# Thresholded attention followed by a leaky-ReLU feed-forward layer: plain DMAs moved from SyncE's queue to GpSimd's, and PV five steps behind the scores in place of four

## The chip, the cores and the metric

The kernel runs on one core of a Trainium2 chip. The metric is the device time of one execution in microseconds (us); the median of several runs is compared. Beside the runs there is one profiled execution, from which every duration of a single instruction comes. The engines are TensorE (PE in the profile; PEld are its weight loads), VectorE (DVE), ScalarE (ACT), GpSimd (POOL) and SyncE (SP), which only issues DMAs here.

## What is computed

The reference, cut to what matters (batch 8, heads 8, sequence 576, head dimension 64, d_model 512, d_ff 2048, tau 0.02):

```python
scores = scale * np.matmul(q, k.transpose(0, 1, 3, 2))
thresh = np.max(scores, axis=-1, keepdims=True) - tau
scores = np.where(scores >= thresh, scores, -1000000000.0)
attn = np.exp(scores - np.max(scores, axis=-1, keepdims=True))
attn = attn / (np.sum(attn, axis=-1, keepdims=True) + 1e-09)
o = np.matmul(attn, v)                 # 8, 8, 576, 64
x = o.transpose(0, 2, 1, 3).reshape(8 * 576, 512)
h = x @ w_in
out = np.maximum(0.01 * h, h) @ w_out  # 4608, 512 in float32
```

## The kernel before

**Steps.** The attention is cut into 144 steps, 18 for each batch. A step is one batch b, one column group c and one pair p. The query rows are split over five column groups: c = 0 to 3 have four steps each, and c = 4 has two. In the last batch the order of the groups is 0, 1, 4, 2, 3. The order of all instructions is written out by hand: the loop at L435 runs over steps s, and each engine executes its own instructions in the order in which the loop emits them. Semaphores are placed where one engine needs another's data or a buffer that is still in use.

**What one step does.** TensorE computes the scores of step s in PSUM (L300, 36 matmuls with q as the weights). VectorE copies them out with their maxima (`smax`, L354, twice), computes the thresholded P for one head (L474) while ScalarE does the other (L476). In the next step VectorE clamps P (L461), ScalarE takes the exponentials into a tile w (L465, four buffers, NW), VectorE writes the reciprocal sums beside them (L480, L481), and `turn_w` (L368) has SyncE issue a DMA that transposes w into wt. LAG steps after the scores, TensorE multiplies wt by v (`pv`, L319). After the last pair of a column group VectorE scales the result out of PSUM (L331, or L336 for c = 4), which makes one group's x ready.

wt is a tile of four slots, one for each pair of a column group, with two buffers (NWT). Its slot 0 is written first; the buffer is free when PV and the evacuation of the column group two before are done.

**The feed-forward layer.** Each group of 128 tokens gives four units of h (16 matmuls, L201, then a ReLU on ScalarE, L214) and four units of o (4 or 5 matmuls). Units wait in two queues, hq and oq, and the loop takes about one of each in a step. At the end of a group, ScalarE copies the output to osb (L243, three buffers), and the store (L244) is issued at the head of the next step. After the loop, a tail works off the units that are left, and VectorE copies their outputs (L241).

**Preparing q and k.** For high precision, q and k are split into a high and a low 16-bit part. `load_half` (L79) loads half of a batch's heads (576 KB) into km or qm. `hi` (L138, on ScalarE) makes the high part, `x64` (L144) and `lo` (L150) on GpSimd make the low part, and `turn` (L154) has SyncE issue a DMA transpose to kst or qst. This is done one batch ahead; the steps at which each part is emitted stand in L389 to L409. GpSimd's arithmetic and its loads of v and of the layer's weights are each made to wait for VectorE's instruction at L461 in the same step (`after_anchor`, L89). Batch 0 is prepared ahead of the loop, with the low part on VectorE.

**DMA queues.** All transposes, the loads of q and k and the stores are issued by SyncE; v, w_in and w_out are loaded by GpSimd. In each step the order on SyncE's queue is: a store, if there is one; turn_w of the step before; then what the table of steps holds (loads, turns). On GpSimd's queue it is what the table of steps holds, in the order in which the table was filled.

Of the kernel before, what the change touches and what calls it, by code (L numbers as in the profile page):

```python
# [16 lines left out]
def kernel(  # L17
# [20 lines left out]
    nc = tc.nc  # L38
# [3 lines left out]
    DM = moe_w_in.shape[0]  # L42
    DF = moe_w_in.shape[1]
    C = 1.0 / (64.0 * 64.0 * 8.0)
    LAG = 4
    L1_GROUPS = set(range(8, 36))
    WIO = 20
    NJ = DF // 128
# [30 lines left out]
    def load_half(src, store, nm, b, hb):  # L79


        m = store[b, hb] = sb.tile([128, 2, 576], FP32, tag=nm, bufs=2, name=nm)
        nc.sync.dma_start(
            out=m, in_=src[b, :, :, :].rearrange("(h f) (p t) d -> f p h (t d)", h=2, t=9)[
                ds(2 * hb, 2)].rearrange("f p h x -> (f p) h x"))

# [112 lines left out]
    tail = [False]  # L199
    def mm(out_, lhsT, rhs, start, stop):  # L200
        nc.tensor.matmul(out=out_, lhsT=lhsT, rhs=rhs, start=start, stop=stop, skip_group_check=True)  # L201
# [21 lines left out]
    def o_unit(G, c):  # L223
        if c == 0:
            n = len(late) % 3 if tail[0] else 2
            late.append(0)
            if n < 2:
                G.op = ps.tile([128, 4, 256], FP32, tag=f"sc{n}", bufs=1, name="op")[:, 0:2, :].rearrange("p a b -> p (a b)")
            else:
                G.op = ps.tile([128, 512], FP32, tag="o", bufs=1, name="op")  # L230
        if G.l1:
            mm(G.op, G.x[:, c, :], w_io16[:, c, :], c == 0, False)
        for j in range(4 * c, 4 * c + 4):
            mm(G.op, G.g[:, j, :], w_out16[:, j, :], j == 0 and not G.l1, j == NJ - 1)
        if c == 3:
            op = G.op

            def fin():
                osb = sb.tile([128, 512], FP32, tag="osb", bufs=3, name="osb")
                if tail[0]:  # L240
                    nc.vector.tensor_copy(out=osb, in_=op)  # L241
                else:
                    nc.scalar.activation(out=osb, in_=op, func=AF.Copy, bias=0.0, scale=1.0)  # L243
                return lambda: nc.sync.dma_start(out=G.rows, in_=osb)  # L244
            return fin
        return None

# [60 lines left out]
    def pv(s):  # L308
        b, c, p = steps[s]
        wt = st[s]["wt"]  # L310
        vt = vts[b]
        n = 128 if c < 4 else 64
        if p == 0:
            pvt[0] = ps.tile([128, NP, n], FP32, tag="pv", bufs=1, name="pv")
        pvp = pvt[0]
        for u in range(1 if c < 4 else 2):
            for j in range(5):
                for h in range(2):
                    nc.tensor.matmul(  # L319
                        out=pvp[ds(64 * h, 64), p + u, :], lhsT=vt[:, p + u, h, j, :],  # L320
                        rhs=wt[:, 4 * h + j, ds(64 * u, n)],
                        start=(j == 0), stop=(j == 4), skip_group_check=True, tile_position=(0, 64 * h))
        last = p == (NP - 1 if c < 4 else NP - 2)
        G, col, done = group_of(b, c)

        def evac():


            if c < 4:
                x_ = G.x.rearrange("f g (p i) -> f g i p", i=2)  # L330
                nc.vector.tensor_tensor(  # L331
                    out=x_, in0=pvp.rearrange("f g (i p) -> f g i p", i=2),
                    in1=wts[0][:, :, 9, :].rearrange("f g (i p) -> f g i p", i=2), op=AX.mult)
            else:
                x_ = G.x.rearrange("f g (p i) -> f g i p", i=2)[:, :, col // 64, :]
                nc.vector.tensor_tensor(  # L336
                    out=x_.rearrange("f (a u) p -> f a u p", u=2),
                    in0=pvp.rearrange("f (a u) p -> f a u p", u=2),
                    in1=wts[0][:, 0:2, 9, :].rearrange("f a (u p) -> f a u p", u=2), op=AX.mult)
            if done:  # L340
                for u in range(4):
                    hq.append((h_unit(G, u), u))

        wts = [st[s]["wt4"]]
        return evac if last else None
# [31 lines left out]
    for hb in range(2):  # L377
        load_half(k, kms, "km", 0, hb)
        load_half(q, qms, "qm", 0, hb)
# [9 lines left out]
    for b in range(1, B):  # L389
        s0 = 18 * (b - 1)  # L390
        for hb in range(2):
            t0 = s0 + PREP + 8 * hb
            at(t0 - 5, lambda b=b, hb=hb: load_half(k, kms, "km", b, hb))
            at(t0 - 3, lambda b=b, hb=hb: load_half(q, qms, "qm", b, hb))
            at(t0 - 1, lambda b=b, hb=hb: hi("k", b, hb))
            at(t0 + 2, lambda b=b, hb=hb: hi("q", b, hb))
            i = 0
            for nm in "kq":
                for h in range(2):
                    at(t0 + i, lambda nm=nm, h=h, b=b, hb=hb: after_anchor(x64(nm, b, hb, h)))  # L400

                    def f(nm=nm, h=h, b=b, hb=hb):
                        for part in PARTS[nm]:
                            after_anchor(lo(nm, b, hb, h, part))
                    at(t0 + i + 1, f)
                    i += 2
                at(t0 + i, lambda nm=nm, b=b, hb=hb: turn(nm, b, hb))
        for i in range(4):
            at(s0 + PREP + 6 + i, lambda b=b, i=i: load_v(b, i))  # L409
# [24 lines left out]
    stores = []  # L434
    for s in range(NS + LAG + 1):  # L435
        live = s < NS
# [21 lines left out]
        if 0 < s <= NS:  # L458
# [5 lines left out]
            for h in range(2):  # L464
                nc.scalar.activation(  # L465
                    out=e["W"][:, ds(576 * h, 576)], in_=e["P"][:, h, :], func=AF.Exp, bias=exp_bias, scale=1.0,
                    accum_out=sm[:, h : h + 1])
        if live:
# [6 lines left out]
                out=d["P"][:, 0, :], in0=sa, scalar1=ma, scalar2=tau_f, op0=AX.subtract, op1=AX.add)  # L475
            nc.scalar.activation(out=d["P"][:, 1, :], in_=sB, func=AF.Identity, bias=bb, scale=1.0)  # L476
        leak()
        if 0 < s <= NS:
# [3 lines left out]
                out=e["W"][:, 1152:1280].rearrange("p (h r) -> p h r", h=2),  # L482
                in0=rc.unsqueeze(2).to_broadcast([128, 2, 64]), scalar1=1.0, scalar2=None, op0=AX.mult)
            turn_w(s - 1)
        evac = None
        if 0 <= s - LAG < NS:
            evac = pv(s - LAG)
        for i, o in enumerate(ou):
# [65 lines left out]
```

## Time and profile before

| What | Value |
|---|---|
| median of 9 runs | 629.73 us (619.21 to 632.48) |
| profiled execution | 626.12 us, span from first to last instruction 624.3 us |
| mean granted TensorE clock in it | 0.969 |
| PE busy | 521.1 us, 83% |
| DVE busy | 445.4 us, 71% |
| ACT busy | 441.9 us, 71% |
| POOL busy | 146.1 us, 23% |
| DMA queue of SyncE (q1, hardware) | 96.50 MB, its packets 86.9% of 16 engines' span |
| DMA queue of GpSimd (q0, software) | 8.92 MB, 11.2% |

A line of a timeline gives the start in us, the length in us, engine, line of the kernel, operation, output<-input and the number of merged instructions; a bracket gives the engine's idle time before it and what ended that. A line of the waits gives who waited for whom, the total in us, how often, and the longest. SPq is SyncE's queue; the length of a DMA there is the time to issue it, not the time to land. The shares of the two DMA queues add up to more than their engines' time where packets of both are under way at once.

### The profile page before, as it was taken

The page shows a single profiled execution, that of the slowest core. Times are in us where ns is not written, and L with a number is a line of the kernel's source. Part 1 is how long each engine was busy: PE and PEld are TensorE (multiplying, and loading weights), DVE is VectorE, ACT ScalarE, POOL GpSimd, SP SyncE. Part 2 cuts the span into 40 slices and gives each one's busy share as a digit, 9 for nine tenths or more (in the row PEclk, how much of TensorE's full clock was granted, in tenths as well). Part 3 has the DMA queues.
Part 4 walks back from the last instruction along what each step waited for, and adds up shares of the span by engine and source line. Part 5 has one row for each costly group of instructions (what it writes and reads, how often), then busy time and mean ns, then how long its engine had stood idle before and what let it go on. Part 6 is the DMA issues. An engine that isn't in the chain of part 4 may idle for free.

```text
span 624.3 us, 23173 instructions
## 1 busy us (share of the span) xinstructions
PE 521.1 (83%) x9840; PEld 374.7 (60%) x9840; DVE 445.4 (71%) x1385; ACT 441.9 (71%) x950; POOL 146.1 (23%) x196
## 2 busy tenths in 40 slices
PE   0442569897897989989897989899998989999997
PEld 0332456664465757767575766676676767677764
DVE  4563459887478878878785878777886868888810
ACT  3352448776468769879786878878887878888831
POOL 0362412123121242124321232124212332000000
PEclk9999979899799889999998999999998989999999
DMA  8899999999969799999999899969998999897821
GB/s 228 186 132 211 205 148 160 209 182 192 189 102 215 128 210 175 219 166 200 197 180 188 152 194 190 219 123 225 189 196 153 208 188 151 154 112 128 128 63 51
DMA packets 299048, 106.90 MB, mean 171 GB/s; under 512 B 273856, under 2 KB 286144, under 8 KB 298944
## 3 DMA queue, kind: packets, MB, share of 16 engines
q1 hardware_dynamic: 285888, 96.50, 86.9%
q0 software_dynamic: 13056, 8.92, 11.2%
q8 instruction: 77, 1.26, 0.9%
q14 instruction: 27, 0.22, 0.1%
HBM read 36.70 MB, written 9.44 MB: 74 GB/s over the span
## 4 chain that ended last, share of the span: by engine, by line
PE 54%; DMA 28%; DVE 12%; ACT 2%; SPq 2%; issue 2%; ACTq 0%; DVEq 0%
DMA wt<-w 20%; PE op L201 19%; PE hp L201 14%; PE sc L300 13%; DMA qst<-qs 7%; PE pv L319 6%; DVE sf L354 6%; PE wiop L201 2%; SPq L156 2%; DVE gT L196 1%; DVE xT L331 1%; DVE P L461 1%; DVE P L474 1%; DMA qm<-in_q_dram 1%; DMA km<-in_k_dram 1%
## 5 line engine op out<-in xcount | busy, mean ns | idle before, releaser
L354 DVE TENSOR_SCALAR_CACHE_REDUCE sf<-sc 128x576 f32<-128x576 f32 x288 | 206.6, 755 | 114.9 <-PE sc L300 113.7
L465 ACT ACTIVATE w<-P 128x576 f16<-128x576 f16 x288 | 193.6, 675 | 26.5 <-DVE P L461 18.3
L300 PE MATMUL sc<-kst,qst 64*64 64x192 f16 x5184 | 147.6, 258 | 42.5 <-DMA kst<-ks 16.2
L201 PEld LDWEIGHTS <-win 128*128 128x128 f16 x2304 | 145.6, 100 | 35.0 <-issue 3.2
L476 ACT ACTIVATE P<-sf,bb 128x576 f16<-128x576 f32 x144 | 111.4, 773 | 70.4 <-DVE bb L472 65.1
L201 PE MATMUL hp<-xT,win 128*128 128x128 f16 x2304 | 157.5, 223 | 0.0
L201 PE MATMUL op<-wout,gT 128*128 128x512 f16 x576 | 152.8, 389 | 0.1
L300 PEld LDWEIGHTS <-qst 64*64 64x64 f16 x5184 | 114.0, 112 | 60.8 <-DMA qst<-qs 32.7
L214 ACT ACTIVATE gT<-hp 128x512 f16<-128x512 f32 x144 | 85.2, 592 | 53.3 <-PE hp L201 50.8
L319 PE MATMUL pv<-wt,v 128*64 128x128 f16 (+1 forms) x1600 | 71.6, 225 | 55.8 <-DMA wt<-w 49.0
L319 PEld LDWEIGHTS <-v 128*64 128x64 f16 x1600 | 51.5, 114 | 76.9 <-issue 54.8
L201 PEld LDWEIGHTS <-gT 128*128 128x128 f16 x576 | 54.8, 100 | 53.9 <-issue 5.5
L474 DVE TENSOR_SCALAR P<-sf,mx 128x576 f16<-128x576 f32 x144 | 73.8, 513 | 0.0
L461 DVE TENSOR_SCALAR P<-P 128x1152 int16<-128x1152 int16 x144 | 66.2, 460 | 9.1 <-ACT P L476 4.0
L150 POOL TENSOR_TENSOR ks<-km,ks 128x320 f16<-128x320 f32 (+1 forms) x56 | 40.1, 736 | 88.6 <-DVE P L461 75.5
L150 POOL TENSOR_TENSOR qs<-qm,qs 128x576 f16<-128x576 f32 x28 | 35.8, 1280 | 86.7 <-DVE P L461 68.5
L465 ACT ACTIVATION_READ_ACCUMULATOR w<-P 128x1 f32 x288 | 54.7, 190 | 0.0
L144 POOL TENSOR_SCALAR km<-km 128x576 f32<-128x576 f32 x28 | 18.8, 672 | 147.0 <-ACT ks L138 101.3
L201 PE MATMUL op<-wio,xT 128*128 128x512 f16 x112 | 44.5, 397 | 0.8 <-ACT osb L243 0.8
L481 DVE TENSOR_SCALAR w<-rc 128x128 f16<-128x128 f32 x144 | 32.9, 229 | 5.0
L144 POOL TENSOR_SCALAR qm<-qm 128x576 f32<-128x576 f32 x28 | 18.8, 672 | 57.1 <-DVE P L461 57.1
L331 DVE TENSOR_TENSOR xT<-pv,wt 128x512 f16<-128x512 f32 x32 | 23.4, 731 | 10.0 <-PE pv L319 10.0
(28 smaller groups left out, 232.7 us busy)
## 6 DMA issues: line engine op xcount, KB each, us to landing
km<-in_k_dram SPq DMA_DIRECT2D x16, 576.0 KB, 5.6
qm<-in_q_dram SPq DMA_DIRECT2D x16, 576.0 KB, 5.5
out_dram<-osb SPq DMA_DIRECT2D x36, 256.0 KB, 4.1
v<-in_v_dram POOLq DMA_DIRECT2D x16, 160.0 KB, 5.8
wt<-w SPq DMA_TRANSPOSE x144, 4.7
v<-in_v_dram POOLq DMA_DIRECT2D x16, 128.0 KB, 5.6
win<-in_moe_w_in_dram POOLq DMA_DIRECT2D x8, 256.0 KB, 13.8
wout<-in_moe_w_out_dram POOLq DMA_DIRECT2D x8, 256.0 KB, 10.4
```

What stands on the lines that cost most here:

```text
L144: return nc.gpsimd.tensor_scalar(out=m, in0=m, scalar1=64.0, scalar2=1.0, op0=AX.mult, op1=AX.mult)
L150: return nc.gpsimd.tensor_tensor(out=dst[:, h], in0=src[:, h], in1=h_[:, h], op=AX.subtract)
L201: nc.tensor.matmul(out=out_, lhsT=lhsT, rhs=rhs, start=start, stop=stop, skip_group_check=True)
L214: nc.scalar.activation(out=gv, in_=hp, func=AF.Relu, bias=0.0, scale=0.99)
L300: nc.tensor.matmul(out=sc[h][ds(64 * u, 64), part, 0:192], lhsT=qsts[b, hb][r, qi, 2 * c + u if c < 4 else 8, ds(64 * g, 64)], rhs=ksts[b, ...
L319: nc.tensor.matmul(out=pvp[ds(64 * h, 64), p + u, :], lhsT=vt[:, p + u, h, j, :], rhs=wt[:, 4 * h + j, ds(64 * u, n)], start=(j == 0), sto ...
L354: nc.vector.tensor_scalar(out=thirds(sf), in0=sc[:, 0:3, 0:192], scalar1=C, scalar2=None, op0=AX.mult, op1=AX.max, accum_out=mx)
L461: anchor[0] = nc.vector.tensor_scalar(out=pi, in0=pi, scalar1=NEG, scalar2=None, op0=AX.max)
L465: nc.scalar.activation(out=e["W"][:, ds(576 * h, 576)], in_=e["P"][:, h, :], func=AF.Exp, bias=exp_bias, scale=1.0, accum_out=sm[:, h : h ...
L474: nc.vector.tensor_scalar(out=d["P"][:, 0, :], in0=sa, scalar1=ma, scalar2=tau_f, op0=AX.subtract, op1=AX.add)
L476: nc.scalar.activation(out=d["P"][:, 1, :], in_=sB, func=AF.Identity, bias=bb, scale=1.0)
L481: nc.vector.tensor_scalar(out=e["W"][:, 1152:1280].rearrange("p (h r) -> p h r", h=2), in0=rc.unsqueeze(2).to_broadcast([128, 2, 64]), sca ...
```

## The change

The loads of q and k for batches 1 to 7 (28 DMAs) and all stores that are issued in the loop or right behind it (33 of 36) are issued by GpSimd's queue; the loads of batch 0, the last stores in the tail and all transposes stay on SyncE. They are not tied to L461. PV runs five steps behind the scores, so that the loop has one step more. Buffer counts and the steps at which loads are emitted stay as they are.

```diff
-    LAG = 4
+    LAG = 5
...
         m = store[b, hb] = sb.tile([128, 2, 576], FP32, tag=nm, bufs=2, name=nm)
-        nc.sync.dma_start(
+        (nc.sync if b == 0 else nc.gpsimd).dma_start(
             out=m, in_=src[b, :, :, :].rearrange("(h f) (p t) d -> f p h (t d)", h=2, t=9)[
                 ds(2 * hb, 2)].rearrange("f p h x -> (f p) h x"))
...
-                return lambda: nc.sync.dma_start(out=G.rows, in_=osb)
+                return lambda: (nc.sync if tail[0] else nc.gpsimd).dma_start(out=G.rows, in_=osb)
```

## The prediction

> **What bounds the kernel now.** I read the chain that ended last first, then the waits in total, then two batches side by side, then SyncE's queue at one stall. The chain, by engine and line:
>
> ```profile
> PE 54%; DMA 28%; DVE 12%; ACT 2%; SPq 2%; issue 2%; ACTq 0%; DVEq 0%
> DMA wt<-w 20%; PE op L201 19%; PE hp L201 14%; PE sc L300 13%; DMA qst<-qs 7%; PE pv L319 6%; DVE sf L354 6%; PE wiop L201 2%; SPq L156 2%; DVE gT L196 1%; DVE xT L331 1%; DVE P L461 1%; DVE P L474 1%; DMA qm<-in_q_dram 1%; DMA km<-in_k_dram 1%
> ```
>
> TensorE is the bound for over half the span, and two transposes by DMA interrupt it: wt (the softmax weights, for PV) and qst (the queries, for the scores). The waits (us in total, times, longest) size that:
>
> ```profile
> PE pv L319 <- DMA wt<-w: 49.0, 19, 7.1
> ...
> PE sc L300 <- DMA qst<-qs: 16.1, 6, 3.7
> ...
> ACT w L465 <- DMA wt<-w: 7.5, 2, 4.6
> ```
>
> Of the 49.0 us, six waits before 83 us make 29.5, two near 150 us make 4.7, and the others, 2.6 us at most, make 14.8. Each of the six for qst stands at the third step of a batch.
>
> Batches 6 and 7 as stretches (start and end, length, busy time of PE, PEld, DVE, ACT, POOL, then clock, DMA share, GB/s); during batch 7 nothing is loaded for a next one:
>
> ```profile
> 462.85:531.21 68.36, 63.78 (x1228) 45.48 (x1226) 52.74 (x168) 54.55 (x119) 18.91 (x24) 0.95 1.03 178
> 531.21:589.25 58.04, 57.09 (x1182) 41.41 (x1181) 49.35 (x159) 48.69 (x108) 0.00 (x0) 1.00 0.82 133
> ```
>
> Batch 7 makes 17 step intervals in 58.04 us with TensorE 98% busy; its undisturbed step is 3.35 us. Eighteen of these are 60.3 us, and batches 2 to 6 take 65.2 to 69.4. TensorE's work is the floor, and about 7 us a batch are stalls on it. SyncE's queue ahead of batch 6's stall, and TensorE at it:
>
> ```profile
> 462.49 0.57 SPq L83 DMA_DIRECT2D qm<-in_q_dram  x1
> 463.24 1.58 SPq L368 DMA_TRANSPOSE wt<-w  x1
> 464.91 4.84 SPq L156 DMA_TRANSPOSE qst<-qs  x1
> ...
> 471.81 0.94 PE L300 MATMUL sc<-kst,qst 64*64 64x192 f16 x36 [2.20 <-DMA qst<-qs]
> ...
> 473.49 1.91 PE L201 MATMUL op<-wout,gT 128*128 128x512 f16 x4
> 475.20 1.72 PE L201 MATMUL hp<-xT,win 128*128 128x128 f16 x16
> ...
> 478.38 1.03 PE L201 MATMUL op<-wout,gT 128*128 128x512 f16 x4
> ```
>
> A load of q goes into the queue 2.4 us ahead of the critical transpose, which then takes 6.85 us to land where an uncontended one (161.53 us) took 4.8. The bracket is TensorE's wait. A stall also costs afterwards: the same four matmuls take 1.91 us behind it and 1.03 a step later, 16 of hp 1.72 in place of 1.06, together 1.5 us more.
>
> **The change, part by part.** The sum is made against the profiled execution: 626.1 us, its span 624.3. The median shown is 629.7, so 3.6 us more.
>
> *PV a step later.* No instruction is added but one drain step. Each wt gets one step, 3.35 us, more until TensorE needs it. Not all of that counts: w has four buffers, so the exponentials of step s+4 (L465) need the transpose of step s landed too, and they start some 0.5 us before PV would now. I take 2.8 us. That covers each of the 14.8 us of small waits and most of the two near 150 us (0.7 and 4.0); with the slow matmuls after three of them, some 6 us, 25.5 us is the most. The startup waits (29.5 us) I leave out: the w buffers hold ScalarE to the same landings there, as its two waits show. The transfers remain and can be late again, so I take 21, bounds 10 and 25.5.
>
> *Loads through GpSimd's queue.* 28 loads of 576 KB leave SyncE. In the trace GpSimd ends the qs subtraction of that step at 458.60 us; its queue then holds the load, which so goes out 3.9 us before SyncE's 462.49. Such a load landed 5.5 us after issue at the median, so it is nearly out of qst's way. Without any load ahead, at the start of batch 7, qst still landed 0.95 us late; that stays. The six waits and the slow matmuls behind five of them (7.5 us by the lengthened next steps) are 23.6 us; less six times 0.95 it is 17.9 at most. At least nothing, if the transfers meet anyway. I take 11, nearer the upper row, because the issue moves by more than the stall.
>
> *SyncE's issue time.* 28 loads at 0.6 us and 33 stores at 0.58 leave a queue that issues for 50 to 58 us of each 65 to 69 us batch. That is some 36 us off SyncE, and shows through the transposes' landing alone, so it is in the two terms above.
>
> *The start.* Now SyncE issues batch 1's first km at 19.88 us, behind the four first turns, and ScalarE waits 4.07 us for it. GpSimd's queue is empty then: it can issue when km's first buffer is free, near 11.4. The first wt then goes some 2.5 us earlier, and the weight loads behind it. Against that, the two loads' 32 packets for each DMA engine (93 ns each in the packet records) are 3 us, and fall among the turns that start the scores. Gain 2.5, bounds -3 and +5.
>
> *GpSimd's work.* 61 DMAs at 0.66 us are 40 us; GpSimd goes from 146 to 186 us busy, hidden in an engine that idles 77% of the time. The meeting with VectorE is not hidden by itself. The nearest rows:
>
> ```profile
> L474 DVE TENSOR_SCALAR P<-sf,mx x144: 507/510/641, 19.4 to 591.8; 128x576 f16<-128x576 f32 x144
> ...
> L461 DVE TENSOR_SCALAR P<-P x144: 440/460/722, 20.4 to 593.2; 128x1152 int16<-128x1152 int16 x144
> ...
> L108 POOL DMA_DIRECT2D v<-in_v_dram x32: 617/658/843, 26.4 to 502.8; - x32
> ```
>
> (min/median/max ns). The worst L461, 722 ns, lies beside a weight load's issue: 0.26 us more. 61 times that is 16 us; VectorE waits 0.41 us a step for the scores, which covers one meeting. I take a loss of 2, bounds 0 and 16.
>
> A store also waits at the head of a step for osb (L243), which ends near 1.2 us into the step; GpSimd's x64 and subtraction queue behind it and come up to 1.9 us later. Their turn follows 5 us or more after them in the steps looked at, so nothing is late next.
>
> The Trainium skill speaks against this part. SBUF — State Buffer, "Who interferes with whom", says that while VectorE is in a two-port mode GpSimd cannot write descriptors, and whoever comes second blocks fully; the advice is to issue from SyncE or ScalarE. The 32 issues of v took 0.62 to 0.84 us although many lay across L474, so the trace shows far less than its example (about 620 ns growing to 3100). By that example each load would only start 2.5 us later, and the sum would lose the 11 of qst and come 11 us higher.
>
> *The longer hold of a wt buffer.* There are two wt tiles, and the fifth column group of a batch has only two steps. So the first turn_w of a batch needs the PV and the evacuation (L331) of three steps before; these now fall one step after its natural place. It waits on SyncE until some 4.2 us into the next step, 4 to 5 us late, and the next two transposes queue behind it. PV needs it three steps on, 11 us, and it lands 8 to 9 us in, so 1.4 to 2.5 us are left: loss 2 in seven batches, bounds 0 and 10.
>
> *Drain.* One more step without scores at 2.5 us, less the scores that now run inside the waits of the start: loss 0.5, bounds -1.7 and +2.5.
>
> Sum: 21 + 11 + 2.5 - 2 - 2 - 0.5 = 30 us. 626.1 - 30 = 596.1, and with the median's offset 599.7; I say 599.
>
> **Rivals.**
>
> *The DMA engines are the bound, and the waits only move.* For it: a DMA share of 1.03 in batch 6. The packet records hold 802 packets of the software queue and 802 of the other between 45 and 50 us, one for one, and there successive wt landed 9.4 us apart: a load on its own queue pushes in between a transpose's packets instead of standing ahead. Against: with transposes alone a packet takes 19.3 ns of an engine, so a batch's work (18 wt of 80, four turns of 144, loads, v and stores) is some 52 of 60.3 us. If only 10 of the first term and none of the second come, 626.1 - 10 - 2.5 + 4.5, with the offset 622. Chance 0.16.
>
> *The held wt buffer decides.* If the first three wt of a batch land 3 us later than I think, each batch gives 3 us back: 7 x 3 = 21 against 30, about 618. For it: landings of 18 us at the longest. Against: that was with the weight loads. Chance 0.06.
>
> *GpSimd's late subtractions lock VectorE: slower.* Behind a store, the 1.28 us subtraction slides from under L354, beside which nothing stretches, onto L474 and L481. If VectorE then waits for all of it, a store costs 1.28 - 0.41, a load 0.66 - 0.41: 33 x 0.87 + 28 x 0.25 = 36 us, and qst's gain goes because GpSimd runs late. 599.7 + 36 + 11 = 647. It passes the old time once a meeting costs VectorE over 0.9 us; the worst row shows 0.26. Chance 0.06.
>
> **How the numbers follow.** My forecast has 0.72. A comparison of this kernel can tell about 2% from no change, 12.6 us, so faster is below 617. Forecast: 0.70 faster, 0.02 within. First rival: 0.05 and 0.11. Second: 0.03 and 0.02, with 0.01 slower. Third: 0.06 slower. That is 0.78, 0.15, 0.07. All good ends together (25.5 + 17.9 + 5) give 581; the upper end takes in most of the first rival. The range is 582 to 621, the forecast's own 585 to 614.
>
> **What would show it.** Right: PE pv waiting for wt falls from 49 us to near the startup's 30; the qst waits fall below 8 us; batches 2 to 6 last 61 to 64 us; qm is issued near the end of L150; L461 stays below 0.75 us at its longest; SyncE waits for L331 at each batch's start. Wrong: batches above 65 us, ScalarE waiting for wt in place of TensorE, VectorE's L474 lengthened by more than 0.4 us at the median, or scores waiting for kst or qst as long as before.

## The result, and the profile after

The changed kernel takes 648.46 us (median of 12 runs, 634.84 to 672.91) where the kernel before takes 629.73 (39 runs beside it). The comparison of the two, which leaves out executions more than 1.5% above the fastest of their kernel (the profiled one of the changed kernel is such a one, 1.8% above), gives a ratio of 1.0216 with a 95% interval of 1.0161 to 1.027: slower by about 2.2%, where 599 us and a gain were forecast. The profiled execution took 646.02 us, its span 644.2, 19.9 us more than that of before.

The chain of waits of the changed kernel, by engine and line:

```profile
PE 48%; DMA 32%; DVE 11%; ACT 5%; issue 2%; SPq 1%; POOL 0%; ACTq 0%; DVEq 0%; POOLq 0%
DMA wt<-w 25%; PE op L201 16%; PE hp L201 12%; PE sc L300 11%; DVE sf L354 6%; PE pv L319 5%; DMA qst<-qs 4%; PE wiop L201 2%; ACT w L465 2%; DMA kst<-ks 1%; DMA winT<-win 1%; ACT P L476 1%; DVE P L461 1%; DVE gT L196 1%; ACT qs L138 1%
```

The transpose of w into wt grew from 20% to 25% of the chain, that of the queries into qst shrank from 7% to 4%. The waits (us in total, times, longest):

```profile
ACT w L465 <- DMA wt<-w: 76.7, 16, 14.5
PE pv L319 <- DMA wt<-w: 73.1, 17, 14.7
...
PE sc L300 <- DMA kst<-ks: 21.0, 1, 21.0
...
PE sc L300 <- DMA qst<-qs: 5.3, 4, 1.9
```

Before, the first scores waited:

```profile
PE sc L300 <- DMA kst<-ks: 16.2, 1, 16.2
```

TensorE's three rows account for nearly the whole loss: PV waits 73.1 - 49.0 = 24.1 us longer, the first scores 21.0 - 16.2 = 4.8 us longer, and the later scores 16.1 - 5.3 = 10.8 us less. That is 18.1 us, and 2.0 us more of PE busy (523.1 against 521.1) make 20.1, against 19.9 measured. The gain on qst came; it was paid for twice over in wt. PV now waits less often than before (17 times against 19) but its longest wait is 14.7 us in place of 7.1.

Batches 6 and 7 as stretches (columns as in the prediction):

```profile
478.90:547.20 68.30, 63.02 (x1227) 45.51 (x1226) 53.06 (x168) 54.62 (x119) 22.66 (x30) 0.95 1.11 186
547.20:606.30 59.10, 57.15 (x1185) 41.45 (x1187) 49.37 (x159) 48.27 (x107) 2.56 (x4) 1.00 0.72 122
```

Batch 6 stays at 68.3 us where 61 to 64 were expected; batches 2 to 6 take 67.7 to 72.8. Batch 7, for which nothing more is loaded, is again near its floor. So the loss sits where q and k are loaded. One such place, on SyncE's queue (the length is the time to issue), on GpSimd, and on TensorE:

```profile
187.06 1.34 SPq L368 DMA_TRANSPOSE wt<-w  x1
188.45 2.58 SPq L156 DMA_TRANSPOSE kst<-ks  x1
191.14 18.42 SPq L368 DMA_TRANSPOSE wt<-w  x4
209.61 2.85 SPq L156 DMA_TRANSPOSE qst<-qs  x1
```

```profile
187.42 1.28 POOL L150 TENSOR_TENSOR qs<-qm,qs 128x576 f16<-128x576 f32 x1 [3.62 <-issue]
188.64 0.77 POOL L83 DMA_DIRECT2D km<-in_k_dram  x1
...
195.20 0.78 POOL L83 DMA_DIRECT2D qm<-in_q_dram  x1
```

```profile
199.68 0.94 PE L300 MATMUL sc<-kst,qst 64*64 64x192 f16 x36
208.13 0.75 PE L319 MATMUL pv<-wt,v 128*64 128x128 f16 x10 [7.51 <-DMA wt<-w]
208.81 1.89 PE L201 MATMUL op<-wout,gT 128*128 128x512 f16 x4
```

GpSimd issues the load of km 0.2 us behind SyncE's transpose to kst. That load lands at 199.12, after 10.5 us, and the transpose at 199.94, after 11.5; the wt behind it is issued from 191.14 and lands at 208.09, after 16.9 us, and TensorE stands still for 7.51 us. This is more than another order of the same transfers: less is moved. The windows give 136 GB/s from 188 to 198 us, with a DMA share of 1.11. Over all stretches from 95 us on in which a load of q or k is under way, the packet records give 183 GB/s, where they give 207 before. The medians from issue to landing say it for all loads:

```profile
km<-in_k_dram POOLq DMA_DIRECT2D x14, 576.0 KB, 7.0
qm<-in_q_dram POOLq DMA_DIRECT2D x14, 576.0 KB, 7.3
```

Before, these were 5.6 and 5.5. Landings of wt over 10 us after the startup (from 95 us on): none before, 11 now. The median landing of kst went from 6.2 to 10.1 us.

### The profile page after: what moved, and what is told of

Same layout as the page of the kernel before. It is cut to its first block, busy times and chain, and to the rows that moved or that the text cites. A ratio compares the mean times of both kernels' runs of the same rounds, so it can differ in the third digit from the quotient of the medians.

```text
span 644.2 us, 23189 instructions
## 1 busy us (share of the span) xinstructions
PE 523.1 (81%) x9840; PEld 375.5 (58%) x9840; DVE 449.6 (70%) x1385; ACT 440.1 (68%) x950; POOL 186.2 (29%) x257
## 3 DMA queue, kind: packets, MB, share of 16 engines
q8 instruction: 77, 1.26, 0.8%
## 4 chain that ended last, share of the span: by engine, by line
PE 48%; DMA 32%; DVE 11%; ACT 5%; issue 2%; SPq 1%; POOL 0%; ACTq 0%; DVEq 0%; POOLq 0%
DMA wt<-w 25%; PE op L201 16%; PE hp L201 12%; PE sc L300 11%; DVE sf L354 6%; PE pv L319 5%; DMA qst<-qs 4%; PE wiop L201 2%; ACT w L465 2%; DMA kst<-ks 1%; DMA winT<-win 1%; ACT P L476 1%; DVE P L461 1%; DVE gT L196 1%; ACT qs L138 1%
## 5 line engine op out<-in xcount | busy, mean ns | idle before, releaser
L201 PEld LDWEIGHTS <-win 128*128 128x128 f16 x2304 | 146.1, 100 | 35.4 <-issue 3.9
L201 PE MATMUL hp<-xT,win 128*128 128x128 f16 x2304 | 158.1, 224 | 0.0
L201 PE MATMUL op<-wout,gT 128*128 128x512 f16 x576 | 154.4, 392 | 0.0
L319 PE MATMUL pv<-wt,v 128*64 128x128 f16 (+1 forms) x1600 | 71.8, 225 | 80.0 <-DMA wt<-w 73.1
L201 PEld LDWEIGHTS <-gT 128*128 128x128 f16 x576 | 54.8, 100 | 54.2 <-issue 6.1
L474 DVE TENSOR_SCALAR P<-sf,mx 128x576 f16<-128x576 f32 x144 | 78.9, 548 | 0.0
L461 DVE TENSOR_SCALAR P<-P 128x1152 int16<-128x1152 int16 x144 | 65.5, 455 | 8.8 <-ACT P L476 5.2
L244 POOL DMA_DIRECT2D out_dram<-osb x33 | 21.2, 642 | 173.7 <-ACT osb L243 173.7
L480 DVE RECIPROCAL rc<-sm 128x2 f32<-128x2 f32 x144 | 22.7, 158 | 62.8 <-ACT w L465 62.4
L150 POOL TENSOR_TENSOR ks<-km,ks 128x320 f16<-128x320 f32 (+1 forms) x56 | 39.9, 733 | 49.3 <-DVE P L461 29.2
L150 POOL TENSOR_TENSOR qs<-qm,qs 128x576 f16<-128x576 f32 x28 | 35.8, 1279 | 56.2 <-issue 28.2
L201 PE MATMUL op<-wio,xT 128*128 128x512 f16 x112 | 44.1, 394 | 0.9 <-ACT osb L243 0.8
```

The costliest lines, as they stand in the source:

```text
L150: return nc.gpsimd.tensor_tensor(out=dst[:, h], in0=src[:, h], in1=h_[:, h], op=AX.subtract)
L319: nc.tensor.matmul(out=pvp[ds(64 * h, 64), p + u, :], lhsT=vt[:, p + u, h, j, :], rhs=wt[:, 4 * h + j, ds(64 * u, n)], start=(j == 0), sto ...
L461: anchor[0] = nc.vector.tensor_scalar(out=pi, in0=pi, scalar1=NEG, scalar2=None, op0=AX.max)
L474: nc.vector.tensor_scalar(out=d["P"][:, 0, :], in0=sa, scalar1=ma, scalar2=tau_f, op0=AX.subtract, op1=AX.add)
L480: nc.vector.reciprocal(out=rc, in_=sm)
```

## The experiments

The theory after the result: the loads on GpSimd's queue slow the transposes that are under way beside them, and are slowed themselves. The rivals: the later PV holds its wt buffer too long and so blocks SyncE's queue; the stores on GpSimd hold up its arithmetic, or VectorE meets GpSimd; the transfers are the bound and any order gives the same. A number of the form a/b is this kernel's median against that of the kernel before, run beside it; a ratio with an interval is made as in the section on the result. Where no interval is given, none was had.

**One part at a time.**

*PV later, alone.*

```diff
-    LAG = 4
+    LAG = 5
```

> The kernel before with PV five steps behind the scores, all DMAs as before on SyncE. Theory A (a load issued by GpSimd, in flight beside a transpose, slows both): faster than before by 5 to 20 us, PE pv waits for wt after the startup near 5 us in place of 19.5, no landing of wt over 10 us after the startup. Theory B (the held wt buffer bunches the transposes, and the drain is longer): slower than before by 10 us or more, with SyncE waiting for L331 some 40 us as in the changed kernel and ScalarE waiting for wt.

Measured: 627.08/628.45 us, ratio 1.0025 (0.9975 to 1.0076). Its waits:

```profile
PE pv L319 <- DMA wt<-w: 36.2, 9, 10.0
...
PE sc L300 <- DMA qst<-qs: 23.8, 7, 4.6
```

PV waits less, as forecast, and nothing is won that can be measured. In the profiled execution (617.72 us, the fastest of the ten), TensorE's idle time ahead of PV after the startup falls from 25.0 to 6.2 us, but ahead of the scores it grows from 17.0 to 24.3, in the startup by 6.0 and ahead of L201 by 1.7, and drain and tail take 2.5 longer (partly the same time): 15 to 17.5 of the 18.8 us go back.

*Loads and stores, PV as before.*

```diff
-        nc.sync.dma_start(
+        (nc.sync if b == 0 else nc.gpsimd).dma_start(
...
-                return lambda: nc.sync.dma_start(out=G.rows, in_=osb)
+                return lambda: (nc.sync if tail[0] else nc.gpsimd).dma_start(out=G.rows, in_=osb)
```

> The changed kernel with PV four steps behind again: loads of batches 1 to 7 and stores on GpSimd's queue. Theory A: slower than before by 3 to 6% (the changed kernel's loss and what the later PV gave it); landings of wt above 10 us beside loads after the startup, first scores at 21 us in place of 16. Theory B: within 1% of before or faster.

Measured: 661.15/628.45, 5.2% slower by the medians, and the spreads don't meet (643.15 to 669.86 against 618.89 to 638.72). The harm comes with the moved DMAs and needs no later PV.

*The loads alone* (the first of these two edits).

> The kernel before with only the loads of batches 1 to 7 on GpSimd's queue. Theory A: nearly all of the loss of loads and stores together, 2 to 5% slower than before, first scores at 21 us. Theory C (GpSimd's queue held up behind the stores, its subtractions late, VectorE stretched): within 1% of before, since no store waits on GpSimd.

Measured: 665.45/628.45, ratio 1.0583 (1.037 to 1.0797).

```profile
PE pv L319 <- DMA wt<-w: 101.2, 25, 13.5
PE sc L300 <- DMA kst<-ks: 21.1, 1, 21.1
...
PE sc L300 <- DMA qst<-qs: 2.1, 2, 1.1
```

All of it is here: PV waits for wt twice as long as before, while qst's 16.1 us are as good as gone.

*The stores alone* (the second edit).

> The kernel before with only the stores on GpSimd's queue. Theory A: within 1.5% of before, as stores are 9.4 of 28 MB and leave less often beside the q and k transposes. Theory C: 2% slower or more, L474 up to 0.9 us as in the changed kernel.

Measured: 629.0/628.45, ratio 1.0016 (0.9955 to 1.0076). The waits of POOL's stores for osb come to 153.1 us there and cost nothing. VectorE does meet GpSimd's late arithmetic in this run: L474 takes up to 1.53 us, beside GpSimd's subtraction (L150), and 595 ns in the mean against 513 before, some 12 us over 144 steps. The expectation had put 0.9 us and 2% on that, and the time shows nothing of it. Stores on GpSimd, and GpSimd's late arithmetic behind them, are not the cause.

**Why loads on that queue cost so much.**

*Streams by themselves.* A kernel of DMAs alone, with nothing of the reference computed: phases of 24 transposes of the size of wt, alone and beside twelve loads of 576 KB (or other DMAs) from one engine's queue.

```diff
+    def phase(n_tr, f=None, eng=None, n=0):
...
+            nc.sync.dma_start(out=wts[i % 4], in_=W, transpose=True)
...
+    phase(24)
+    phase(24, load, nc.sync, 12)
+    phase(24, load, nc.scalar, 12)
+    phase(24, load, nc.gpsimd, 12)
+    phase(24, load_pad, nc.gpsimd, 12)
+    phase(24, store, nc.gpsimd, 12)
+    phase(24, load_v, nc.gpsimd, 24)
```

> Computes nothing of the reference: nine phases, one after the other, each a stream of 24 transposes of 128x1280 from SyncE (as wt) with a second stream beside it: none; 12 loads of 576 KB from SyncE; the same from ScalarE; the same from GpSimd; from GpSimd into rows with a gap (so that two rows of 2304 bytes are not one run of 4608); 12 stores of 256 KB from GpSimd; 24 loads of v with a cast from GpSimd; then 12 loads alone from GpSimd and from SyncE. Theory S (GpSimd's loads beside transposes slow both): phase 4 lasts 1.4 times phase 2 or more, phase 3 as long as phase 2. Theory Q (any second queue does it): phases 3 and 4 both last 1.4 times phase 2. Theory T (it is the moment of issue in the kernel, not the queue): phases 2, 3 and 4 within 10% of each other. Theory P (the size of the packets): phase 5 short where phase 4 is long.

Measured once, in us for a phase: transposes alone 39.6; with loads from SyncE 64.0, from ScalarE 58.3, from GpSimd 73.7 (67.1 into a tile with gaps); with GpSimd's stores 49.8, with its 24 loads of v 58.2. The windows from the start of a phase until its last load landed (transposes alone; ScalarE; GpSimd; the columns are DVE and POOL busy, clock, DMA share, GB/s):

```profile
14.10:53.70 39.60, 0.55 (x6) 0.00 (x0) 1.00 1.06 199
...
121.40:163.50 42.10, 0.15 (x10) 0.00 (x0) 1.00 1.10 274
181.60:241.10 59.50, 0.10 (x3) 8.78 (x12) 1.00 1.13 202
```

In this run the same twelve loads are through in 42.1 us from ScalarE's queue and in 59.5 from GpSimd's, at 274 and 202 GB/s with the DMA engines equally busy. VectorE does almost nothing in either, so no meeting of VectorE and GpSimd is needed for such a loss. GpSimd's phase is 1.26 times ScalarE's and 1.15 times SyncE's, where 1.4 times SyncE's was expected. A second run below does not repeat the 202 GB/s.

*The loads on ScalarE's queue, PV as before.*

```diff
-        nc.sync.dma_start(
+        (nc.sync if b == 0 else nc.scalar).dma_start(
```

> The kernel before with the loads of batches 1 to 7 issued by ScalarE's queue in place of SyncE's. Theory Q: slower than before by 4% or more, as with GpSimd's queue, kst's transpose at 9 us or more at the median. Theory S: within 1.5% of before, kst near 6 us. Theory T: slower where the loads leave early, beside kst's transpose.

Measured: 617.13/631.21, ratio 0.9811 (0.9682 to 0.9939). These loads are issued 0.1 to 0.2 us into their steps, GpSimd's in the run with the loads alone 2.2 to 2.4 us into the step before, some 1.2 us earlier; in the run with GpSimd's loads a step later (below) they come after ScalarE's. On either side of ScalarE's moment GpSimd's queue loses, 5.8% and 2.2%, and ScalarE's gains 1.9%.

```profile
PE pv L319 <- DMA wt<-w: 64.9, 23, 10.5
...
PE sc L300 <- DMA qst<-qs: 2.6, 3, 1.1
```

The wait for qst goes here too, and no wt takes over 10 us to land after the startup. One part of the expectation is missed: kst lands after 8.8 us at the median, not near 6 (6.2 before, 9.4 with the loads alone on GpSimd's queue). So ScalarE's loads slow kst as well; what they lack is the late wt behind it. The idea of the change, loads off SyncE's queue, is sound; GpSimd's queue at the steps that were kept is not.

*The loads on GpSimd into a tile whose rows have a gap*, meant to make two small packets of each large one (GpSimd's loads have packets of 4608 bytes, SyncE's of 2304).

```diff
-        m = store[b, hb] = sb.tile([128, 2, 576], FP32, tag=nm, bufs=2, name=nm)
-        nc.sync.dma_start(
+        m = store[b, hb] = sb.tile([128, 2, 584], FP32, tag=nm, bufs=2, name=nm)[:, :, 0:576]
+        (nc.sync if b == 0 else nc.gpsimd).dma_start(
```

> Loads of batches 1 to 7 on GpSimd's queue, into tiles whose two rows have a gap between them, so that packets are of 2304 bytes and not 4608. Theory P: within 2% of before. Theories S and T: 4 to 7% slower, as with loads alone on GpSimd's queue.

Measured: 674.11/631.21, ratio 1.0641 (1.0454 to 1.0828). The packets stayed at 4608 bytes, so this run repeats the loads alone and says nothing of the size of packets.

*The loads on GpSimd a step later.*

```diff
-            at(t0 - 5, lambda b=b, hb=hb: load_half(k, kms, "km", b, hb))
-            at(t0 - 3, lambda b=b, hb=hb: load_half(q, qms, "qm", b, hb))
+            at(t0 - 4, lambda b=b, hb=hb: load_half(k, kms, "km", b, hb))
+            at(t0 - 2, lambda b=b, hb=hb: load_half(q, qms, "qm", b, hb))
```

> Loads of batches 1 to 7 on GpSimd's queue, emitted one step later, so that they leave about when SyncE sent them before. Theory T: within 2% of before, landings of wt above 10 us gone. Theories S and P: still 4 to 7% slower, with landings of wt above 10 us.

Measured: 640.47/631.21, ratio 1.022 (1.0101 to 1.034). The same queue at another moment costs 2.2% in place of 5.8%: the moment matters as well as the queue. Four landings of wt after the startup are still above 10 us, where 9 were with the loads alone.

*Streams by themselves, other packets.* The kernel of DMAs again, with loads of one row a partition (twice as many, 288 KB) and with one load in flight at a time.

```diff
+    phase(24, load, nc.gpsimd, 12)
+    phase(24, load_row, nc.gpsimd, 24)
+    phase(24, load_one, nc.gpsimd, 12)
+    phase(24, load, nc.scalar, 12)
+    phase(24, load_row, nc.scalar, 24)
+    phase(24, load_one, nc.scalar, 12)
```

> Computes nothing of the reference: streams of 24 transposes of 128x1280 from SyncE, one after the other: alone; beside 12 loads of 576 KB from GpSimd with two in flight; beside 24 of half the size (one row of 2304 bytes a partition) from GpSimd; beside 12 from GpSimd with one in flight; then the same three from ScalarE; at the end 12 loads from ScalarE alone. Theory S (GpSimd's queue itself): all three GpSimd phases 1.15 times or more of ScalarE's like ones. Theory P (packets of 4608 bytes, which only GpSimd's loads show): the phase with single rows falls to ScalarE's length, within 5%. If it is the number in flight: the phase with one load in flight falls to ScalarE's length.

Measured once, GpSimd against ScalarE: 58.7 against 55.3 us (1.06 times), 68.7 against 55.7 with loads of one row (1.23 times), 64.5 against 59.4 with one in flight (1.09 times). Only one of the three reaches the 1.15 times that was expected of theory S. GpSimd's first phase took 73.7 us in the other run with the same DMAs. Here its loads were through in 41.4 us at 275 GB/s, ScalarE's in 39.0 us at 296. So GpSimd's phase is the longer one each time, but a large loss of throughput is not there each time, and what decides on it the streams don't show. Theory P stays untested: the packet records of this run show 4608 bytes in all three of GpSimd's phases, that of single rows too, and 2304 in all of ScalarE's.

**Where the rest of the forecast went.**

*The kernel before with the load of q three steps earlier*, on SyncE's queue as it was.

```diff
-            at(t0 - 3, lambda b=b, hb=hb: load_half(q, qms, "qm", b, hb))
+            at(t0 - 6, lambda b=b, hb=hb: load_half(q, qms, "qm", b, hb))
```

> The kernel before, all DMAs on SyncE, with the load of q emitted three steps earlier, so that it no longer stands just ahead of the critical qst. If the qst waits come from that load, as the prediction had it: TensorE's late waits for qst fall from 17 us below 8 and the time by 1 to 2%. If they come from SyncE's queue and the transfer itself: qst waits as before, time within 1%.

Measured: 610.73/628.83, and in a second set below 610.58/630.49, ratio 0.9728 (0.9642 to 0.9814).

```profile
PE pv L319 <- DMA wt<-w: 55.3, 22, 7.7
...
PE sc L300 <- DMA qst<-qs: 5.9, 5, 1.8
```

So the stall that the prediction read at 462 us was what it seemed: the load ahead of qst on the same queue. Taken away by one number, it is worth 2.7%, over 17 us, with no change of queue, more than the 1 to 2% that were expected. In the profiled executions, 15.1 us apart in span, the waits for qst are 10.2 us less, PE busy falls from 521.1 to 512.3 us, and PV waits 6.3 us longer.

*PV later, with a third buffer for wt.*

```diff
-    LAG = 4
+    LAG = 5
...
-    NWT = 2
+    NWT = 3
```

> PV five steps behind and three wt buffers in place of two, all DMAs on SyncE. If the held wt buffer is what ate the gain of the later PV: SyncE's 39 us of waiting for L331 are gone and the time is 1 to 3% below before. If the gain went to the qst waits and the longer drain: within 1% of before, as with the later PV alone.

Measured: 634.81/628.83. SyncE's wait for L331 (39.0 us with LAG alone) is gone from the profile, and the time is no better; TensorE still idles 29.4 us ahead of the scores after the startup. The held buffer costs nothing that can be seen by itself.

*Loads on ScalarE, PV later, three buffers* (the edits of those runs together).

> Loads of batches 1 to 7 on ScalarE's queue, PV five steps behind, three wt buffers. If the queue was the fault and the rest of the forecast held: 3 to 5% below before, waits of PV for wt after the startup under 10 us. If the DMA engines are the bound: no better than ScalarE's loads alone, about 2% below.

Measured: 625.61/628.83, no better than ScalarE's loads alone. PV waits less (12.5 us of idle time after the startup against 33.4 with ScalarE's loads alone), the scores more (20.1 against 2.6). Again the later PV moves waits from one transpose to the other.

*The loads on GpSimd, clear of the turns*: at steps at which they land before the next transpose to kst or qst starts.

```diff
-            at(t0 - 5, lambda b=b, hb=hb: load_half(k, kms, "km", b, hb))
-            at(t0 - 3, lambda b=b, hb=hb: load_half(q, qms, "qm", b, hb))
+            at(t0 - (5 if hb else 7), lambda b=b, hb=hb: load_half(k, kms, "km", b, hb))
+            at(t0 - (1 if hb else 3), lambda b=b, hb=hb: load_half(q, qms, "qm", b, hb))
```

> Loads of batches 1 to 7 on GpSimd's queue, emitted at steps from which they should land before the next kst or qst goes out (k of the first half two steps earlier, q of the second half two steps later). If the cost is the meeting with kst and qst: within 1.5% of before, kst near 6 us. If a load on this queue costs beside any transpose: still 3 to 6% slower, with landings of wt above 10 us.

Measured: 613.74/630.49, ratio 0.9819 (0.9744 to 0.9894), where the same loads on the same queue cost 5.8% at their old steps.

```profile
PE pv L319 <- DMA wt<-w: 53.0, 22, 9.6
...
PE sc L300 <- DMA kst<-ks: 21.5, 1, 21.5
...
PE sc L300 <- DMA qst<-qs: 5.6, 5, 2.0
```

```profile
km<-in_k_dram POOLq DMA_DIRECT2D x14, 576.0 KB, 5.8
qm<-in_q_dram POOLq DMA_DIRECT2D x14, 576.0 KB, 6.1
```

Counted from 45 us on, a load is under way beside a transpose to kst or qst for over 1 us 3 times in 25 here, and 16 times in 24 with the loads alone. In that run the 16 took 8.7 us at the median (14.3 at the longest), the other 8 took 5.7; in the changed kernel 17 took 9.1 and 7 took 6.3. On SyncE's queue before, 15 that met took 5.9 and 11 others 5.2. So GpSimd's loads cost where they meet the large transposes at the old steps, and nothing where they are clear of them. A meeting alone is not the whole condition: ScalarE's loads meet one 13 times in 25 at a gain, and GpSimd's loads a step later 17 times in 25, then land after 6.3 us and cost 2.2%. While loads are under way after 95 us, the packet records give 175 GB/s with the loads alone on GpSimd, 214 a step later, 204 clear of the turns, 221 from ScalarE and 207 before: the case with the large loss is the one where less is moved. Which detail of the old moment does it is not shown; there GpSimd issues 8 of the 24 loads 0.2 to 0.4 us behind a transpose to kst or qst, which it does with none a step later, nor does ScalarE. No run has ScalarE's loads at that distance, so how much of the 5.8% is the queue's and how much the moment's stays open. The start's loss is still there (21.5 us to the first scores) and is more than made good. Two landings of wt after the startup are above 10 us, 12.1 at the longest.

*PV later and q earlier, on SyncE (both edits as above); and q earlier again.*

> PV five steps behind and q's load three steps earlier, all DMAs on SyncE. If the later PV's gain was eaten by the qst waits: PV's late waits below 10 us and those for qst below 10 us, 595 to 603 us, 1 to 2% under the earlier load of q alone. If it is eaten by the start and the drain, or by waits that only move: no faster than the earlier load of q alone, 607 to 615.

> The load of q three steps earlier alone, as e8, beside the one above on one chip: 2 to 3.5% below before, with an interval.

Measured: 612.13/630.49 with both, 610.58/630.49 with q earlier alone. The later PV adds nothing even where the load is out of qst's way. The last has the lowest median of all and beats both kernels; from the version with both (601.04 to 616.3) and from GpSimd's loads clear of the turns (613.19 to 614.32) its spread, 605.42 to 618.43, does not set it apart.

## Why the prediction was wrong, step by step

**What bounds the kernel: right in part.** The reading that the six waits for qst come from the load just ahead is shown by the run with q earlier. That time is won by letting PV come later is shown wrong: the idle time ahead of PV does go, and comes back elsewhere.

**"Loads through GpSimd's queue" is the step that failed.** It forecast +11, bounds 0 and 17.9. The gain is there (qst's waits 16.1 to 5.3 us), but the step says "at least nothing, if the transfers meet anyway", and this lower bound left out a loss. The prediction had computed the earlier moment of issue and looked only at what it gets out of the way of. It did not ask which transfer runs at the new moment: the transposes to kst and qst. Alone, this edit costs 665.45 - 628.45 = 37 us where +11 was in the sum. The step also took 5.5 us, the landing on SyncE's queue, for a load on another queue; 7.0 and 7.3 were measured. The trace of before held a warning: beside GpSimd's loads of the layer's weights in the startup, wt took up to 18.55 us to land. The prediction saw it, in its second rival, and set it aside as a matter of the weight loads; it did not ask whether loads of q and k from the same queue would do the same.

**"PV a step later" failed too; it was put at 21.** Its first half works, TensorE's idle time ahead of PV falls by 18.8 us, but its worth alone is nothing measurable (1.0025). Beside the slow loads and stores it may be worth something: 661.15 us without it and 648.46 with it, though the spreads overlap, and TensorE's idle time ahead of PV after the startup falls from 69.2 to 45.8 us. Neither the held buffer nor the load of q explains why the scores then wait longer, and a slow transfer doesn't either: in the two runs that have the later PV and the load of q out of the way (from ScalarE with three buffers, or earlier on SyncE), the qst at the third step of batches 1 to 6 lands 4.7 to 5.8 us after its issue, near the 4.8 of an uncontended one, and TensorE still waits 2.8 to 3.9 us for all of them but one. These transposes are not slow; they are sent too late for a TensorE that no longer stands at PV. That fits the first rival, in which TensorE only comes sooner to the next transpose. No run sends the turns earlier, so what that would be worth is open. (The term's upper bound, 25.5, also counts the wait of 4.0 us whole where 2.8 us were credited.)

**"The start" had the wrong sign.** Forecast +2.5, bounds -3 and +5; the first scores come 4.8 us later. The two loads that GpSimd issues at 10.66 and 11.53 us meet the first transpose to kst, which lands at 20.92 in place of 16.16: the failure of the loads' step once more, at a place where all of it is on the path. The prediction had priced this meeting at 3 us.

**"GpSimd's work" held.** POOL is busy 186.2 us, as forecast. The durations (min/median/max ns) of the two lines of VectorE:

```profile
L461 DVE TENSOR_SCALAR P<-P x144: 439/459/486, 25.1 to 609.7; 128x1152 int16<-128x1152 int16 x144
```

```profile
L474 DVE TENSOR_SCALAR P<-sf,mx x144: 508/510/884, 24.2 to 608.8; 128x576 f16<-128x576 f32 x144
```

The meeting moved from L461 to L474, 0.37 us more at the worst, its mean 548 in place of 513 ns: 5 us over 144 steps, in an engine with room. The rule of the Trainium skill that the prediction weighed, SBUF — State Buffer, "Who interferes with whom", does not explain the loss: issues of the loads took 0.74 to 0.87 us, and a loss also appears in the first run of streams, where VectorE idles. The lock itself fits what the run with the stores alone shows, L474 at up to 1.53 us beside GpSimd's subtraction; it cost no time there.

**"The longer hold of a wt buffer" came as described and cost nothing that can be seen.** On SyncE:

```profile
SPq L368 <- DVE xT L331: 43.9, 8, 6.6
```

That is one wait a batch, up to 6.6 us; with a third buffer it goes and the time stays.

**"Drain"** took 37.9 us with the tail in place of 35.1, just past its bound of 2.5.

**The rivals.** The first was nearest in kind (transposes and loads get in each other's way, and the waits for wt move to qst) and wrong in size, since it let waits only move; throughput is lost as well. Of it, the Trainium skill, DMA: Bandwidth & Descriptors, "Issuing engines are not separate DMA queues", says that DMAs of all issuers share the same engines and that another issuer saves only the time to initiate. These runs don't fit the second half: the same loads cost -1.9% from ScalarE, and from GpSimd +5.8%, +2.2% or -1.8% by the moment. The second rival is refuted by the third buffer (its 618 also leaves out the median's offset: 599.7 + 21 is 621). The third named the right side for the wrong reason: the lock that it described does come (L474 up to 1.53 us with the stores alone), but it costs no time, and 33 of its charges were on the stores. No case held a loss from the loads' own transfers: of the chance of 0.07 for slower, 0.06 rested on VectorE and 0.01 on the held buffer. That slower came is no merit of either.

## What to carry to other kernels

When a transfer is moved to another queue, work out which transfers will run beside it at its new moment, and leave room for a loss there; a time to land that was measured on one queue at one moment need not hold for another. Before changing queues, try to move the load: here one number, three steps earlier, brought 2.7%, and the better choice of queue 1.9%. And before giving a consumer a longer lead, look at what it will wait for next.

## What was not expected of the hardware

Loads on GpSimd's queue beside transposes can bring down the throughput of both: in one run of streams 202 GB/s against 274 from ScalarE's queue, with DMA shares of 1.13 and 1.10, so a busy DMA share does not show it. In the other run of the same streams it was 275 against 296. In the kernel it was 175 GB/s at the old steps and 204 to 214 at others, so it goes by the moment as well as by the queue. What inside the DMA engines makes the difference was not settled: one load in flight did not remove it, and packets of 2304 bytes were never had from GpSimd's queue. In a profile it is seen at the issues on SyncE: a transpose of w takes 1.34 us to issue ahead of the meeting and 18.42 for four behind it.
